# Per-token convolution taps softmaxed once in their own slots, and turned into band matrices by 32x32 transposes

## The chip, the cores and the metric

The kernel runs on one core of a Trainium2 chip. The metric is the time of one execution on the device, in microseconds (us). A core has a matrix engine (PE, with its weight loads shown apart as PEld), three engines for elementwise work (DVE, ACT, POOL) and a queue, SP, that issues the DMA transfers. Each engine works through its own list of instructions in order; semaphores make one engine wait for another.

## What is computed

Two steps over 8 sequences of 3584 tokens with 192 channels. First a dynamic convolution: each token and head has its own 7 taps, softmaxed over the 7, and mixes the token with the 6 before it in the same sequence.

```python
w = weight_gen - np.max(weight_gen, axis=-1, keepdims=True)
w = np.exp(w)
w = w / (np.sum(w, axis=-1, keepdims=True) + 1e-09)
x_unf = x_pad[:, idx, :].reshape(B, S, K, H, group)     # B 8, S 3584, K 7, H 8, group 24
out = np.einsum('bshk,bskhg->bshg', w, x_unf).reshape(B, S, D)
```

Then a soft mixture of experts over all 28672 tokens: `logits = x @ phi` (32 slots), a softmax over the tokens gives each slot's input, 8 experts (192 to 1024 to 192, ReLU) transform 4 slots each, and a softmax over the slots gives each token its mix of the outputs. All data are fp32.

## The kernel before

**Tiling.** Tokens are cut into blocks of T = 26, four blocks make a group of 104 tokens, and a sequence has 35 groups (the last one overlaps, its repeats are zeroed later), 280 in all. Two groups are a pair, two pairs a slot of the loop (`SLOTS` = 70), and eight pairs a unit (two short units of six at the end). A block with its 6 tokens of history fills 32 rows of a quarter of the partitions; the four quarters hold four heads.

**Convolution of a pair.** `conv` multiplies, for each block, a band matrix of 128 x 26 (rows: 4 heads x 32 input tokens; columns: the output tokens; each column has its 7 taps on the diagonal band) with the block's x, laid out block-diagonally by head (`big`, called `xbd`; its other quadrants are zeroed once at the start): 16 matrix products in fp32, which the trace shows as 32 matmul instructions. The x of each head carries a 25th column of ones (GX = 25), so the product's 25th column is the sum of the unnormalised taps. `conv_sum` (ACT) reads those sums, `conv_inv` (DVE) inverts them, and `conv_out` (DVE) scales the result on its way from PSUM (`cv`) to SBUF (`tm`).

**Making a band.** The taps come from DRAM twice, once by token (26 rows of 32) and once already spread along the diagonals. `tap_top` (DVE) takes each token's maximum, `tap_spread` (POOL) lays the maxima out, and `tap_rows`, a matmul with the 0/1 matrix `near` into `pmx`, carries each maximum to the rows of the band where that token's taps stand; `tap_sub` (DVE) subtracts it, `tap_exp` (ACT) exponentiates, and `band_make` (POOL) multiplies with a mask into the band. One such chain serves a load of 7 groups (1.75 slots); there are 40.

**The rest of a slot.** `xpose` (PE) transposes the convolved pair in three pieces into `pt`, `xpose_out` (ACT) copies them to `cm`; once per unit `logits` (PE into `ls`), `top`, `newmax`, `newmax_out`, `dexp`, `dturn` and `fade` (a running maximum and exponentials over tokens), `dispatch` (PE into `acb`) and `rescale` (DVE). `soft` and `turn` prepare the softmax over slots. After the loop come the experts and the outputs, which are copied out of PSUM and written by DMA.

**What sets the order.** The opening, up to pair 1, is written by hand. Everything after goes through a planner (`op` and `model`): each operation is listed with an engine, a cost and the buffers it reads and writes; PE's and SP's order is the listed one, and for DVE, ACT and POOL the planner picks by estimated due times. So a changed cost or a changed list moves instructions on those three engines.

Of the kernel before, what the change touches and what calls it, by code (L numbers as in the profile page):

```python
# [16 lines left out]
GX = GW + 1  # L17
# [3 lines left out]
SGG = 7  # L21
# [4 lines left out]
TAPS = NBC * KT  # L26
# [15 lines left out]
def conv_soft_moe(ctx, tc, xh, wh, phi, w1a, w1b, w2, out):  # L42
# [15 lines left out]
    NXH, HBC = 5, NBC // 2  # L58
    XB = 4 * HBC * GX
    big = keep.tile([128, NXH * XB], F32, name="big")  # L60
# [43 lines left out]
    NTM, NCV, NTAP, NBAND = 2, 3, 4, 3  # L104
    xbd = big.rearrange("p (i h c) -> p i h c", i=NXH, h=4)
    HB = NBC // 2


    taps = [fix.tile([128, 2, TAPS], F32, name=f"taps{i}") for i in range(NTAP)]
    bands = [fix.tile([128, T, NBC], F32, name=f"band{i}") for i in range(NBAND)]  # L110
# [5 lines left out]

    pmx = ps_l.tile([128, 512], F32, name="pmx")
    topP = pmx[:, 0:TAPS].rearrange("p (q l) -> p q l", q=KT)
# [7 lines left out]
    one = keep.tile([128, 1], F32, name="one")  # L126
# [11 lines left out]
    V.memset(one, 1.0)  # L138
    V.memset(xbd[:, 0:2, 0], 0.0)
    G.memset(xbd[:, 0:2, 1], 0.0)  # L140
    V.memset(xbd[:, 0:2, 2], 0.0)
    A.copy(xbd[:, 0:2, 3], zero.unsqueeze(1).to_broadcast([128, 2, HBC * GX]))
    ident = keep.tile([128, 128], F32, name="ident")
    make_identity(nc, ident)
    near = keep.tile([128, 128], F32, name="near")
    G.memset(near, 1.0)
    G.affine_select(out=near, in_=near, compare_op=ALU.is_ge, fill=0.0, base=0,
                    pattern=[[1, 128]], channel_multiplier=-1)
    G.affine_select(out=near, in_=near, compare_op=ALU.is_ge, fill=0.0, base=KT - 1,
                    pattern=[[-1, 128]], channel_multiplier=1)  # L150
    mask = keep.tile([128, 1, 32], F32, name="mask")
    maskT = keep.tile([128, 1, 32], F32, name="maskT")
    mask2 = keep.tile([128, 32, 1], F32, name="mask2")
    own = keep.tile([128, KT, 1], F32, name="own")

# [7 lines left out]
    eps = keep.tile([128, 1], F32, name="eps")  # L163
    V.memset(eps, EPS)
    for t in cvs:

        A.copy(t[:, 0 : 16 * GX], one.to_broadcast([128, 16 * GX]))

    def loadx(j):

        s, part = divmod(j, 2)
        z = slice(part * HBC * GX, (part + 1) * HBC * GX)
        for h in range(4):
            SY.dma_start(xbd[32 * h : 32 * h + 32, j % NXH, h], xh[s, h, :, z])  # L174

    def loadw(s):
        SY.dma_start(taps[s % NTAP], wh[s])

    tops = {}

    def tap_top(s):

        tops[s] = pa.tile([128, NBC, 1], F32, tag="top", name=f"top{s}")
        V.tensor_reduce(out=tops[s][:, :, 0], op=ALU.max, axis=AX.X,  # L184
                        in_=taps[s % NTAP][:, 0].rearrange("p (l k) -> p l k", k=KT))

    def tap_spread(s, eng=G):

        tops[s] = pa.tile([128, KT, NBC], F32, tag="spread", name=f"spread{s}"), tops[s]
        eng.tensor_tensor(out=tops[s][0], in0=own.to_broadcast([128, KT, NBC]),  # L190
                          in1=tops[s][1].rearrange("p l o -> p o l").to_broadcast([128, KT, NBC]),
                          op=ALU.mult)

    def tap_rows(s):

        P.matmul(pmx[:, 0:TAPS], near, tops[s][0].rearrange("p q l -> p (q l)"),  # L196
                 start=True, stop=True)

    def tap_sub(s):
        r = taps[s % NTAP][:, 1]  # L200
        V.tensor_tensor(out=r, in0=r, in1=pmx[:, 0:TAPS], op=ALU.subtract)  # L201

    def tap_exp(s):
        A.activation(taps[s % NTAP][:, 1], taps[s % NTAP][:, 1], AF.Exp)  # L204

    def band_make(s, lo=0, hi=HB, eng=G):

        l = slice(2 * lo, 2 * hi)
        r = taps[s % NTAP][:, 1].rearrange("p (q l) -> p q l", q=KT)[:, :, l]
        w = bands[s % NBAND]  # L210
        for j, n in ((0, 3 * KT), (3 * KT, T - 3 * KT)):
            k = min(n, KT)
            eng.tensor_tensor(out=w[:, j : j + n, l].rearrange("p (a k) l -> p a k l", k=k),  # L213
                              in0=r[:, 0:k].unsqueeze(1).to_broadcast([128, n // k, k, 2 * (hi - lo)]),
                              in1=mask2[:, j : j + n].rearrange("p (a k) o -> p a k o", k=k)
                              .to_broadcast([128, n // k, k, 2 * (hi - lo)]), op=ALU.mult)
# [11 lines left out]
    def conv(p):  # L228
        cv = cvs[p % NCV]
        for par in range(2):  # L230
            s, g = divmod(2 * p + par, SGG)
            for c in range(2):
                for blk in range(4):
                    bc = (4 * g + blk) * 2 + c
                    o = 4 * GX * (2 * par + (c ^ par))
                    j, b = divmod(s * NBC + bc, HBC)
                    P.matmul(cv[32 * blk : 32 * blk + T, o : o + 4 * GX],  # L237
                             bands[s % NBAND][:, :, bc],
                             xbd[:, j % NXH, :, b * GX : (b + 1) * GX], start=True, stop=True)

    wss = {}

    def conv_sum(p):

# [706 lines left out]
```

## Time and profile before

| | |
|---|---|
| time, median of 3 runs | 343.48 us (343.11 to 344.02) |
| the profiled execution, first to last instruction | 345.3 us |
| PE, share of the span with a matmul | 89% |
| DVE, POOL, ACT | 72%, 58%, 47% |
| conv loop (first conv to last) | about 8.6 to 258.3 us |
| experts | about 267 to 282 us |
| output writes | about 284 to 345 us |

The profile page gives only the span of the profiled execution; what may lie around it in a timed run is not on the page, and the span is 1.8 us above the median of the runs. Its rows read: line, engine, operation, output tile <- input tiles, shapes, xcount, then busy time, mean ns of one instruction, and the idle time before the instructions with what ended it. Busy time counts overlapping instructions once, so count times mean can be more than busy.

### The profile page before, as it was taken

To read this page: it belongs to the slowest core of one execution; us is meant where nothing else is said; L and a number is where in the kernel's file an instruction comes from. 1 tells how busy PE (TensorE), PEld (TensorE's weight loads), DVE (VectorE), ACT (ScalarE), POOL (GpSimd) and SP (SyncE) were. 2 spreads that over 40 slices of the span, in tenths; PEclk is the share of its full clock that TensorE was granted. 3 is DMA by queue.
4 is the path that set the end of the run, shared out by engine and by line. 5 is a ranking of instruction groups with operands and counts; after the bars stand their busy time and mean duration, and the time that the engine had idled before them with its cause. 6 is when DMAs were issued, how large, how long until landed. Compare 5 with 4: busy or idle time off the path is not lost.

```text
span 345.3 us, 16352 instructions
## 1 busy us (share of the span) xinstructions
PE 306.8 (89%) x6896; PEld 222.2 (64%) x6896; DVE 249.9 (72%) x550; ACT 161.7 (47%) x428; POOL 198.8 (58%) x261
## 2 busy tenths in 40 slices
PE   8789999899999998999999999899997988799600
PEld 6567777687778876778778777678784952124100
DVE  7766877878788886897887868777864759965400
ACT  6535454455645654456445544454632237534300
POOL 8679648679489785868778568586601720000000
PEclk9999999999999999999999999999999999975555
DMA  6787788877877777677876867966589009999995
GB/s 197 215 260 196 214 223 196 246 205 221 215 217 228 211 235 189 199 207 205 241 210 176 237 173 204 260 172 180 154 307 364 6 2 398 395 403 399 395 404 204
DMA packets 33001, 80.82 MB, mean 234 GB/s; under 512 B 7072, under 2 KB 7456, under 8 KB 32928
## 3 DMA queue, kind: packets, MB, share of 16 engines
q1 hardware_dynamic: 32928, 79.77, 74.7%
q8 instruction: 55, 0.90, 1.2%
q14 instruction: 18, 0.15, 0.2%
HBM read 57.38 MB, written 22.36 MB: 231 GB/s over the span
## 4 chain that ended last, share of the span: by engine, by line
PE 58%; DMA 19%; DVE 9%; ACT 4%; issue 3%; SPq 2%; POOL 1%; DVEq 0%; ACTq 0%; POOLq 0%
PE cv L237 25%; PE pt L272 12%; DMA taps<-wh 8%; DMA out<-big 7%; PE pmx L196 6%; PE ls L301 6%; PE acb L365 5%; DMA big<-xh 4%; DVE big L841 3%; PE hpb L765 2%; PE so L786 2%; DVE cT L455 1%; DVE top L184 1%; SPq L174 1%; DVE tm L258 1%
## 5 line engine op out<-in xcount | busy, mean ns | idle before, releaser
L213 POOL TENSOR_TENSOR band<-taps,mask 128x588 f32<-128x588 f32 (+3 forms) x158 | 121.3, 798 | 31.9 <-ACT taps L204 23.1
L237 PE MATMUL cv<-big,band 128*26 128x100 f32 x4480 | 120.4, 252 | 6.2 <-POOL band L213 1.5
L237 PEld LDWEIGHTS cv<-big,band 128*26 128x26 f32 x4480 | 101.0, 128 | 36.4 <-issue 29.0
L258 DVE TENSOR_TENSOR tm<-cv,ws 128x384 f32<-128x384 f32 x140 | 72.9, 551 | 6.7 <-DVE ws L253 1.0
L277 ACT COPY cm<-pt 128x312 f32<-128x312 f32 x140 | 51.9, 423 | 44.5 <-PE pt L272 44.0
L247 ACT ACTIVATE ws<-cv,eps 128x16 f32<-128x16 f32 x140 | 37.7, 272 | 58.0 <-PE cv L237 46.2
L272 PE MATMUL pt<-ident,tm 122*128 122x122 f32 x420 | 59.2, 277 | 0.7 <-ACT cm L277 0.7
L272 PEld LDWEIGHTS pt<-ident,tm 122*128 122x128 f32 x420 | 43.4, 141 | 16.4 <-issue 9.9
L253 DVE RECIPROCAL ws<-ws 128x32 f32<-128x32 f32 x70 | 24.3, 348 | 29.9 <-ACT ws L247 29.4
L190 POOL TENSOR_TENSOR spread<-own,top 128x392 f32<-128x392 f32 x37 | 31.2, 843 | 24.3 <-DVE top L184 13.0
L834 PE MATMUL po<-cT,so 32*128 32x468 f32 (+3 forms) x256 | 38.1, 726 | 5.2 <-DVE big L841 4.5
L841 ACT COPY big<-po 128x936 f32<-128x936 f32 (+2 forms) x25 | 22.4, 902 | 27.1 <-PE po L834 15.2
L196 PE MATMUL pmx<-spread,near 128*128 128x392 f32 x80 | 33.7, 503 | 1.6 <-POOL spread L190 0.8
L841 DVE COPY big<-po 128x884 f32<-128x884 f32 (+2 forms) x24 | 25.4, 1071 | 12.8 <-DMA out<-big 10.5
L834 PEld LDWEIGHTS po<-cT,so 32*128 32x128 f32 (+1 forms) x256 | 12.4, 188 | 29.7 <-DVE big L841 23.1
L184 DVE TENSOR_REDUCE top<-taps 128x56 f32<-128x392 f32 x40 | 22.1, 551 | 12.3 <-DMA taps<-wh 11.2
L301 PE MATMUL ls<-cm,phi_sb 128*32 128x208 f32 (+1 forms) x576 | 29.5, 334 | 0.3 <-issue 0.3
L204 ACT ACTIVATE taps<-taps 128x392 f32<-128x392 f32 x40 | 21.0, 525 | 17.5 <-DVE taps L201 14.5
L365 PE MATMUL acb<-tm,dt 128*32 128x193 f32 x536 | 26.6, 328 | 0.7 <-DVE dt L346 0.4
L301 PEld LDWEIGHTS ls<-cm,phi_sb 128*32 128x32 f32 x576 | 19.9, 109 | 4.6 <-issue 0.6
L201 DVE TENSOR_TENSOR taps<-taps,pmx 128x392 f32<-128x392 f32 x40 | 22.1, 553 | 0.4 <-PE pmx L196 0.4
L92 POOL TENSOR_TENSOR LT<-LT,sm 128x576 f32<-128x576 f32 (+1 forms) x16 | 18.1, 1132 | 5.1 <-DVE sm L90 4.9
(113 smaller groups left out, 256.0 us busy)
## 6 DMA issues: line engine op xcount, KB each, us to landing
big<-xh SPq DMA_DIRECT2D x320, 87.5 KB, 3.9
taps<-wh SPq DMA_DIRECT2D x40, 392.0 KB, 4.6
out<-big SPq DMA_DIRECT2D x23, 468.0 KB, 6.5
out<-big SPq DMA_DIRECT2D x24, 442.0 KB, 6.4
big<-w SPq DMA_DIRECT2D x8, 768.0 KB, 6.9
w1a_sb<-w1a SPq DMA_DIRECT2D x16, 256.0 KB, 3.9
w1b_sb<-w1b SPq DMA_DIRECT2D x8, 256.0 KB, 3.7
out<-big SPq DMA_DIRECT2D x2, 234.0 KB, 2.4
```

Of the source, the lines that this page charges most:

```text
L190: eng.tensor_tensor(out=tops[s][0], in0=own.to_broadcast([128, KT, NBC]), in1=tops[s][1].rearrange("p l o -> p o l").to_broadcast([128, KT ...
L196: P.matmul(pmx[:, 0:TAPS], near, tops[s][0].rearrange("p q l -> p (q l)"), start=True, stop=True)
L213: eng.tensor_tensor(out=w[:, j : j + n, l].rearrange("p (a k) l -> p a k l", k=k), in0=r[:, 0:k].unsqueeze(1).to_broadcast([128, n // k, k ...
L237: P.matmul(cv[32 * blk : 32 * blk + T, o : o + 4 * GX], bands[s % NBAND][:, :, bc], xbd[:, j % NXH, :, b * GX : (b + 1) * GX], start=True, ...
L247: A.activation(wss[p // 2][:, p % 2], cvs[p % NCV][:, 0 : 16 * GX].rearrange("p (h w) -> p h w", w=GX)[:, :, GW:], AF.Identity, bias=eps[: ...
L258: V.tensor_tensor(out=tms[u % NTM][:, pr, 1 : 2 * D + 1].rearrange("p (h w) -> p h w", w=GW), in0=cv[:, :, 0:GW], in1=wss[p // 2][:, p % 2 ...
L272: P.transpose(pt[:, i, 0:TR], tm[0:TR, pr, 1 + 128 * i : 129 + 128 * i], ident[0:TR, 0:TR])
L277: copy(cms[u][:, pr].rearrange("p i b j -> p (i b) j"), pts.pop(p).rearrange("p i (b j) -> p (i b) j", j=32)[:, :, 0:T])
L301: P.matmul(lp[32 * blk : 32 * blk + 32, 0:n, par, 0:T], phi_sb[:, 2 * par + i, :], cm[:, 0:n, 1 if i else 2 * par, blk, :], start=(i == 0) ...
L365: P.matmul(ac[32 * q : 32 * q + 32], dt[:, g, :], tm[:, g // 2, o : o + D + 1], start=(g < 4), stop=(g + 4 >= 2 * n))
L834: P.matmul(po[dst : dst + hi - lo, at, 0 : n * T], so[32 * q : 32 * q + 32, lo:hi], cT[32 * q : 32 * q + 32, g0 : g0 + n, 0:T], start=True ...
L841: (V.tensor_copy if done[1] % 2 else A.copy)(ot.rearrange("p (q c) -> p q c", c=n * T), po[:, 0 : len(qs), 0 : n * T])
```

## The change

**Taps.** They are loaded once, as [partition = head and slot of a group, 2 x 7 taps x 26 tokens]; a load ("chunk", CH = 2) serves 8 groups, two slots of the loop, and there are 35. An eighth row, set to 1e-9 once, stands in for the epsilon of the sum. Per chunk the chain is now `tap_top` (DVE), `tap_sub` (POOL), `tap_exp` (ACT), `tap_sum` (three adds on POOL, folding eight rows to one), `tap_inv` (DVE), `tap_mul` (POOL; writes the softmaxed taps into `wide` at a stride of 33 elements, so that tap k of token j stands at column k + j of row j of a 32 x 32 block), and `tap_turn` (DVE; 32x32 transposes of 128 x 1664 elements from `wide` into the band). `near`, `mask`, `own`, `tap_spread`, `tap_rows` with `pmx`, and `band_make` are gone. `wide` is one buffer; its zeros outside the bands are set once.

**Convolution.** x has no column of ones (24 columns a head, 96 instead of 100 per matmul), `conv_sum` and `conv_inv` are gone, and `conv_out` is a plain copy on ACT. There are four `cv` buffers in place of three. x is loaded by 5 groups (SGG = 5, four buffers) instead of by halves of 7 groups (five buffers): 224 transfers of 32 x 960 elements instead of 320 of 32 x 700.

**Opening.** The first chunk goes through the chain in two halves (LO, HI), partly on DVE; the zeroing of the later x buffers (`clear`) is spread over DVE, POOL and ACT between these steps. The weights of the experts' second layer (`loadw2`) go into x buffers as the last four fall free. In the planner, `dispatch` stands behind a slot's transposes, and for the unit before the first short one it comes a slot later.

```diff
+    def tap_sub(c, b=ALL, eng=G):
+        t = taps[c % NTAP][:, b, 0:KT]
+        eng.tensor_tensor(out=t, in0=t, in1=each(tops.pop((c, b.start)), b.stop - b.start),
+                          op=ALU.subtract)
+    def tap_sum(c, b=ALL, eng=None):
...
+        eng.tensor_tensor(out=s, in0=t[:, :, 0:4], in1=t[:, :, 4:8], op=ALU.add)
+        eng.tensor_tensor(out=s[:, :, 0:2], in0=s[:, :, 0:2], in1=s[:, :, 2:4], op=ALU.add)
+        eng.tensor_tensor(out=m, in0=s[:, :, 0], in1=s[:, :, 1], op=ALU.add)
+    def tap_mul(c, b=ALL, eng=G):
...
+        dst = bass.AP(w.tensor, w.offset, [w.ap[0], [T * 32, n], [1, KT], [33, T]])
+        eng.tensor_tensor(out=dst, in0=taps[c % NTAP][:, b, 0:KT],
+                          in1=each(m, n), op=ALU.mult)
+    def tap_turn(c, b=ALL):
+        V.transpose(bands[c % NBAND][:, b].rearrange("p b j l -> p (b j l)"),
+                    wide[:, b].rearrange("p b j -> p (b j)"))
...
-    def conv_sum(p):
-    def conv_inv(k):
-    def conv_out(p):
...
-        V.tensor_tensor(out=tms[u % NTM][:, pr, 1 : 2 * D + 1].rearrange("p (h w) -> p h w", w=GW),
-                        in0=cv[:, :, 0:GW], in1=wss[p // 2][:, p % 2].to_broadcast([128, 16, GW]),
-                        op=ALU.mult)
+    def conv_out(p, copy=A.copy):
+        copy(tms[u % NTM][:, pr, 1 : 2 * D + 1], cvs[p % NCV][:, 0 : 2 * D])
...
     loadw(0)
+    loadx(0)
     loadw(1)
...
+    tap_top(0, LO)
+    tap_sub(0, LO, V)
+    tap_exp(0, LO)
+    tap_top(0, HI)
+    tap_sub(0, HI)
+    clear_cv(0)
     tap_top(1)
+    tap_exp(0, HI)
+    clear_cv(1)
+    G.memset(wide[:, 0], 0.0)
+    tap_sum(0, LO)
+    tap_inv(0, LO)
+    tap_mul(0, LO, V)
+    tap_sub(1)
+    G.memset(wide[:, 1], 0.0)
+    tap_turn(0, LO)
+    tap_exp(1)
...
+    tap_sum(1, ALL, G)
+    make_identity(nc, ident)
+    clear(2, 2, G)
+    tap_inv(1)
+    tap_mul(1, LO)
+    tap_mul(1, HI)
...
+    clear(2, 3, G)
...
+    loadx(2)
+    for h in range(4):
+        clear(3, h, G)
+    loadx(3)
...
-            dispatched[k0 + 3 if n == UP else k0 + 2] = u - 1
+            dispatched[k0 + 3] = u - 1
...
+    def chain(c):
+        w = ("w", c % NTAP)
+        op(VE, 0.56, [w], [("top", c % 2)], tap_top, c)
+        op(PO, 0.85, [("top", c % 2)], [w], tap_sub, c)
+        op(AC, 0.47, [], [w], tap_exp, c)
+        op(PO, 1.05, [w], [("sum", c % 2), "fold"], tap_sum, c, ALL, G)
+        op(VE, 0.5, [], [("sum", c % 2)], tap_inv, c)
+        op(PO, 0.85, [("sum", c % 2), w], ["wide"], tap_mul, c)
+        op(VE, 1.88, ["wide"], [("band", c % NBAND)], tap_turn, c)
...
+                if t + NXS < NSG:
+                    op(SP, 2.0, [], [x_of(t)], loadx, t + NXS, late=3.0)
+                else:
+                    i = t + NXS - NSG
+                    op(SP, 1.2, [], [x_of(t)], loadw2, i * XB // WE, min((i + 1) * XB // WE, E))
...
-        steps = [(xpose, a - 2), (xpose, b - 2)] + ([(tap_rows, rowed[k])] if k in rowed else [])
...
+        for i in (a - 2, b - 2):
+            op(TE, 0.34, [tm_of(i)], [("pt", i % 2)], xpose, i)
+            op(AC, 0.4, [], [("pt", i % 2), ("cm", unit(i)[1])], xpose_out, i)
```

**Where instructions move.** On PE, slots 4 and 5 of the loop, counted from 0. `cv` is the convolution, `pt` the transposes, `pmx` the matmul of the maxima, `ls` the logits. Before:

```order
L237 MATMUL cv_96<-big,band_90 26x100 x16
L237 MATMUL cv_94<-big,band_90 26x100 x16
L272 MATMUL pt_504<-ident,tm_91 128x122 x3
L272 MATMUL pt_511<-ident,tm_91 128x122 x3
L196 MATMUL pmx<-spread_500,near 128x392
L237 MATMUL cv_95<-big,band_90 26x100 x8
L237 MATMUL cv_95<-big,band_88 26x100 x8
L237 MATMUL cv_96<-big,band_88 26x100 x16
L301 MATMUL ls<-cm_324,phi_sb 32x8x26 x16
```

and now:

```order
L231 MATMUL cv_95<-big,band_91 26x96 x16
L231 MATMUL cv_96<-big,band_91 26x96 x16
L249 MATMUL pt_472<-ident,tm_92 128x122 x3
L249 MATMUL pt_481<-ident,tm_92 128x122 x3
L231 MATMUL cv_97<-big,band_91 26x96 x16
L231 MATMUL cv_98<-big,band_91 26x96 x16
L278 MATMUL ls<-cm_305,phi_sb 32x8x26 x16
```

The `pmx` matmul is gone, a pair no longer straddles two bands, and the rest of PE's order is kept but for `dispatch`, which now follows a slot's transposes and stood ahead of them.

On DVE, the stretch around the first running maximum (`mx` and `mq` are `top`, `nm` is `newmax_out`, `dt` is `dturn`, `LT` is `save`). Before:

```order
L308 TENSOR_REDUCE mx_596<-ls 128x1
L310 TENSOR_SCALAR mq<-acb,mx_596 128x4
L258 TENSOR_TENSOR tm_92<-cv_96,ws_557 128x384
L328 TENSOR_REDUCE nm_647<-acb 128x1
L330 TENSOR_TENSOR mq<-nm_647,acb 128x1
L253 RECIPROCAL ws_644<-ws_644 128x32
L258 TENSOR_TENSOR tm_92<-cv_94,ws_644 128x384
L346 STREAM_TRANSPOSE dt_690<-dd 128x512
```

and now:

```order
L196 RECIPROCAL sum_0_523<-sum_0_523 128x52
L285 TENSOR_REDUCE mx_552<-ls 128x1
L287 TENSOR_SCALAR mq<-acb,mx_552 128x4
L209 STREAM_TRANSPOSE band_90<-wide 128x1664
L305 TENSOR_REDUCE nm_635<-acb 128x1
L307 TENSOR_TENSOR mq<-nm_635,acb 128x1
L196 RECIPROCAL sum_0_578<-sum_0_578 128x52
L323 STREAM_TRANSPOSE dt_660<-dd 128x512
```

The scalings and inversions of pairs have left; the long transposes of the band now stand between `top` and `newmax_out`, and the inversion ahead of `mx` waits for POOL's sums.

On POOL in the opening, from the sums of the second chunk to the band of the third:

```order
L192 TENSOR_TENSOR sum_0_171<-si 128x52
masks.py:197 MEMSET ident 128x128
masks.py:199 AFFINE_SELECT ident<-ident 128x128
L358 MEMSET big 128x960
L204 TENSOR_TENSOR wide<-taps_85,sum_0_171 128x7x26 x2
L358 MEMSET big 128x960 x5
L420 MEMSET selE_126 128x128
L421 MEMSET dd 128x384
...
L176 TENSOR_TENSOR taps_86<-taps_86,top_0_278 128x2x182
L176 TENSOR_TENSOR taps_87<-taps_87,top_0_301 128x2x182
L190 TENSOR_TENSOR si<-taps_86 128x208
L191 TENSOR_TENSOR si<-si 128x2x52
```

Before, the same stretch held the zeroing of x (five `MEMSET` instructions) and then at once the bands of loads 1 and 2; now six of the zeroing instructions of the third and fourth x buffer stand around the products of the second chunk and ahead of the third chunk's subtraction.

More of the change, by code (lines that the diff above doesn't have):

```diff
@@ L137, in conv_soft_moe @@
     warm(0)
[L138 to L142, printed above, removed]
-    ident = keep.tile([128, 128], F32, name="ident")
[L144 to L154, printed above, removed]
+    ident = keep.tile([128, 128], F32, name="ident")
+    eps = keep.tile([128, 1], F32, name="eps")
+    V.memset(xbd[:, 0, 0], 0.0)
+    G.memset(xbd[:, 0, 1], 0.0)
+    A.copy(xbd[:, 0, 2], zero.to_broadcast([128, NBC * GW]))
+    V.memset(xbd[:, 0, 3], 0.0)
+    for t in taps:
+        V.memset(t[:, :, KT], EPS)
+    V.memset(eps, EPS)
     sel4 = keep.tile([128, 4, NS], F32, name="sel4")
@@ L194, in tap_rows, with loadx @@
[L194 to L216, printed above, removed]
+    def loadx(t):
+        for h in range(4):
+            SY.dma_start(xbd[32 * h : 32 * h + 32, t % NXS, h], xh[t, h])
@@ L556, in conv_soft_moe @@
[L556 to L565 removed]
+            op(TE, 0.75 if p == a else 0.72, conv_reads(p), [("cv", p % NCV)], conv, p)
```

278 lines of the change are left out of this document (106 added, 172 removed).

## The prediction

> **What bounds the kernel now.** I read the summary first, then the busy times of the long middle of the program, then the chain of waits there, and last the durations by shape.
>
> ```profile
> span 345.3 us, 16352 instructions
> PE 306.8 (89%) x6896; PEld 222.2 (64%) x6896; DVE 249.9 (72%) x550; ACT 161.7 (47%) x428; POOL 198.8 (58%) x261
> ```
>
> No engine is full over the span, but the share averages an opening, a loop and an output stage that is limited by its writes. The conv loop decides. Its first regular slot (slot 4, counted from 0) starts at 24.06 us, its last convolution ends at 258.34. The row for that stretch, with busy us of PE, PEld, DVE, ACT and POOL in this order, then clock, DMA share and GB/s:
>
> ```profile
> 24.06:258.34 234.28, 228.48 (x5878) 178.89 (x5878) 185.38 (x438) 118.72 (x354) 169.80 (x209) 1.00 0.76 212
> ```
>
> PE works 228.5 of 234.3 us (97.5%), DVE 79%, POOL 72%, ACT 51%. 66 slots in 234.3 us make 3.55 us a slot. The chain of waits in the loop, in order of time (start, us, what), runs on PE from one piece to the next without a gap:
>
> ```profile
> 107.79 1.31 PE acb L365 x24
> 109.10 0.78 PE pt L272 x6
> 109.88 0.67 PE pmx L196 x2
> 110.54 1.54 PE cv L237 x64
> 112.08 0.77 PE pt L272 x6
> 112.86 1.70 PE cv L237 x64
> 114.56 1.41 PE ls L301 x32
> ```
>
> So a slot costs PE 1.54 us of convolution and 0.78 of transposes, a unit's logits (ls) 1.41 and its dispatch (acb) 1.31, and each maxima matmul (pmx) 0.67 that nothing overlaps. How many of each there are says the grouping of the same stretch by line:
>
> ```profile
> L196 PE MATMUL pmx<-spread,near 128*128 128x392 f32 x71 | 29.6, 497 | 0.8 <-POOL spread L190 0.8
> L301 PE MATMUL ls<-cm,phi_sb 128*32 128x208 f32 (+1 forms) x544 | 27.8, 336 | 0.0
> L365 PE MATMUL acb<-tm,dt 128*32 128x193 f32 x512 | 24.9, 328 | 0.7 <-DVE dt L346 0.4 <-issue 0.2
> L324 PE MATMUL acb<-mq,sel 128*32 128x5 f32 (+1 forms) x136 | 3.8, 173 | 1.0 <-DVE mq L310 1.0
> ```
>
> That is 35 pmx of two records (the 71st is cut by the window's edge), 17 logits, 16 dispatches. 66 x 2.32 + 17 x 1.41 + 16 x 1.31 + 3.8 + 35 x 0.67 = 153.1 + 24.0 + 21.0 + 3.8 + 23.5 = 225.4 us. The other 8.9 us are waits.
>
> **The change, part by part.** *PE loses the maxima matmul*: 35 x 0.67 = **23.5 us** of the loop, straight off the bound if nothing else takes its place. (By the group's busy time, which counts overlap with its neighbours, it would be 29.6; the chain's 0.67 is what the next convolution waits.)
>
> *The convolution narrows from 100 to 96 columns.* ls takes 1.41 / 32 = 44 ns an instruction for 208 columns, acb 1.31 / 32 = 41 ns for 193: both 0.212 ns a column. At that rate 100 columns would take 21 ns; the convolution takes 1.54 / 64 = 24.1. Something other than columns paces it, so I count **0**. The ends are a gain of 4% of 66 x 1.54, 4.1 us, and, since the weights are now read at a step of 32 elements instead of 56, which no row shows, a loss of as much.
> The Trainium skill (TensorE: Matmul & The Clock Gate, section "Wait — 56ns, not 53.3ns?") says that matmuls never start closer than about 25 ns, however few columns they have. By that rule the narrowing brings nothing, which goes with the 24.1; without it the sum would be 4.1 us lower.
>
> *The other engines.* Durations by shape (busy, mean ns of one):
>
> ```profile
> L258 DVE TENSOR_TENSOR tm<-cv,ws 128x384 f32<-128x384 f32 x140 | 72.9, 551 | 6.7 <-DVE ws L253 1.0
> L253 DVE RECIPROCAL ws<-ws 128x32 f32<-128x32 f32 x70 | 24.3, 348 | 29.9 <-ACT ws L247 29.4
> L90 DVE RECIPROCAL sm<-sm 128x18 f32<-128x18 f32 x8 | 2.1, 262 | 1.7 <-ACT sm L88 1.5
> L201 DVE TENSOR_TENSOR taps<-taps,pmx 128x392 f32<-128x392 f32 x40 | 22.1, 553 | 0.4 <-PE pmx L196 0.4
> L184 DVE TENSOR_REDUCE top<-taps 128x56 f32<-128x392 f32 x40 | 22.1, 551 | 12.3 <-DMA taps<-wh 11.2 <-POOL band L213 1.1
> L346 DVE STREAM_TRANSPOSE dt<-dd 128x512 f32<-128x512 f32 x16 | 11.3, 706 | 0.2
> L390 DVE STREAM_TRANSPOSE maskT<-mask 128x32 f32<-128x32 f32 x1 | 0.2, 206 | 0.0
> L308 DVE TENSOR_REDUCE mx<-ls 128x1 f32<-128x416 f32 x16 | 9.3, 581 | 1.1 <-PE ls L301 1.0
> L310 DVE TENSOR_SCALAR mq<-acb,mx 128x4 f32<-128x4 f32 x17 | 3.8, 222 | 0.6
> L277 ACT COPY cm<-pt 128x312 f32<-128x312 f32 x140 | 51.9, 423 | 44.5 <-PE pt L272 44.0
> L841 ACT COPY big<-po 128x936 f32<-128x936 f32 x12 | 11.3, 939 | 9.3 <-PE po L834 5.2 <-DMA out<-big 4.0
> L247 ACT ACTIVATE ws<-cv,eps 128x16 f32<-128x16 f32 x140 | 37.7, 272 | 58.0 <-PE cv L237 46.2 <-PE acb L324 5.3 <-DVE taps L201 3.7
> L204 ACT ACTIVATE taps<-taps 128x392 f32<-128x392 f32 x40 | 21.0, 525 | 17.5 <-DVE taps L201 14.5 <-DMA big<-xh 2.8
> L213 POOL TENSOR_TENSOR band<-taps,mask 128x588 f32<-128x588 f32 x77 | 91.0, 1182 | 31.6 <-ACT taps L204 22.8 <-issue 8.1
> L213 POOL TENSOR_TENSOR band<-taps,mask 128x140 f32<-128x140 f32 x77 | 32.6, 423 | 0.0
> L190 POOL TENSOR_TENSOR spread<-own,top 128x392 f32<-128x392 f32 x37 | 31.2, 843 | 24.3 <-DVE top L184 13.0 <-DMA big<-xh 4.2 <-PE acb L324 4.2
> ```
>
> DVE loses in the loop 132 scalings, 66 inversions, 35 subtractions and 35 maxima: 72.7 + 23.0 + 19.4 + 19.3 = 134 us. It gets, for each of 33 chunks, a maximum over 364 elements (0.55, as for 392), an inversion of 52 (6.1 ns an element between 18 and 32: 0.47) and a transpose of 1664 (1.04 ns an element between 32 and 512: 706 + 1152 x 1.04 = 1.90 us): 2.92 x 33 = 96. It ends near 147 of some 210 us, 70%. ACT loses 132 x 0.272 + 35 x 0.525 = 54 and gets 132 copies of 384 (0.827 ns an element between 312 and 936: 0.48) and 33 exponentials of 364 (0.50): 80; near 145, 69%. POOL loses 35 spreads and 35 double bands of two instructions a half (29.5 + 112.4) and gets, at 186 ns + 1.69 an element (from 140 and 588), a subtraction and a product of 364 (0.80 each) and adds of 208, 104 and 52 (0.54 + 0.36 + 0.27): 2.77 x 33 = 91; near 119, 57%. No row has a POOL write at a stride of 33. I take 0.80; the other end, twice that, puts POOL at 70%, still covered. All these lie beside PE, and cost nothing as long as PE's own queue of work hides them.
>
> A chunk's chain, 0.55 + 0.80 + 0.50 + 1.17 + 0.47 + 0.80 + 1.90 = 6.2 us, has four slots, 12.7 us, before its band is needed. DMA gets lighter: taps once instead of twice, and fewer, larger transfers of x. The last expert's weights (w2) now wait for the last x buffer, that is for the end of the convolutions at 258.3 in the old times.
>
> ```profile
> big<-w SPq DMA_DIRECT2D x8, 768.0 KB, 6.9
> 275.32 1.30 PE so L786 x32
> ```
>
> They land in 6.9 us, and the product that reads them begins 17 us after the last convolution, with the other experts first: hidden, by 10 us. `dispatch` behind the transposes instead of ahead is the same work for PE.
>
> *Waits.* Of the 8.9 us, 0.8 (pmx on spread, above) leave with the matmul. The rest I keep: 8.1.
>
> *The opening.* Rows of before in order of time (start, us):
>
> ```profile
> 0.81 0.86 SPq L177 DMA_DIRECT2D taps<-wh  x2
> 2.48 4.09 SPq L174 DMA_DIRECT2D big<-xh  x8
> 4.11 0.55 DVE L184 TENSOR_REDUCE top<-taps 128x56 f32<-128x392 f32 x1
> 7.09 1.26 POOL L396 MEMSET big<- 128x1400 f32 x1
> 8.30 1.30 POOL L398 MEMSET big<- 128x700 f32 x2
> 8.56 0.92 PE L237 MATMUL cv<-big,band 128*26 128x100 f32 x32
> 13.62 0.20 POOL L430 MEMSET selE<- 128x128 f32 x1
> 14.35 0.48 POOL L436 MEMSET qneg<- 32x1 f32 x4
> ```
>
> Taps land 3.3 us after their issue. The second chunk's are now issued behind four x transfers (0.5 each, and they wait for zeroed buffers), near 4.0, and land near 7.3; DVE has that chunk's maximum listed ahead of the first half's sums, so it stands until then. 0.55, then sum 0.36, inversion 0.31, product 0.36 and transpose 1.04 of a half bring the first convolution to about 10.0 (8.56 before); the second half follows at 12.0, the second chunk's inversion at 12.5. Behind it stand, on POOL, two products (0.5 each, 13.5), five zeroings of 960 (0.89 each by the 700 and 1400 above, 18.0), the small ones (13.62 to 14.83 above, 1.2: 19.2), two subtractions (20.8), the sums (22.0), after the inversion (0.5) the product (23.3); then DVE's transpose (25.2). Slot 4 waits for it: 25.3 against 24.06, **+1.2**. Ends: -1.5 if taps land as soon as they can and POOL takes a tenth less, +4 if a transfer of the fourth x buffer, issued at 18, is late.
>
> **Sum**: 345.3 - 23.5 - 0.8 + 1.2 = 322.2 for the profiled execution. That execution was 1.8 us above the median of the runs (343.48), so **320.5 us** for the time, 6.7% less.
>
> **Rivals.** *New waits in the loop* (330): running maxima need `top`, 0.58 + 0.22 us, within the 1.55 us that PE spends on transposes and one convolution after the logits. A 1.90 us transpose that has just begun when the logits end makes PE wait up to 1.15 us; 17 units, at most 19.6. ACT, with 69% on PE's own path (convolution, copy, transposes), can do alike. For: both instructions sit where they didn't. Against: DVE's share falls, and in the order shown the transpose follows `mq`. Half of the most, +9.8.
>
> *Less than counted* (312): the convolution gains its 4.1 and half of the waits go, since DVE and POOL have more slack.
>
> *The matmul's time isn't won* (336): PE drops its 23.5 us, but the loop is paced by what feeds it, say the chunk's chain across three engines, and keeps two thirds of it. Against: 97.5% PE.
>
> *Slower* (355): POOL's product at stride 33 is far dearer than 0.80. Two slots now take 2 x (201.9 + 8.1) / 66 = 6.4 us; POOL has besides the product 1.97 a chunk and (169.8 - 141.9) / 33 = 0.85 of other work. From 3.5 us on the product sets the pace, from 4.3 us (two slots in 7.1 us, as before) the loop is no faster than it was. At 4.6 us it takes 33 x 7.42 = 244.9 instead of 210.0: 322.2 + 34.9 - 1.8 = 355. Against: that is 12.6 ns an element, and spreads (843 ns for 392) take 2.15.
>
> **How the numbers follow.** Forecast 0.60, new waits 0.17, less than counted 0.12, not won 0.06, slower 0.05. The likeliest gives 320.5. The range, 311 to 331, takes in the third case and most of the second. 0.3% (1.0 us) is what a measurement here can tell: faster 0.94, the same 0.01, slower 0.05.
>
> **What would show it.** Right: pmx gone from PE; PE busy over 95% between slot 4 and the last convolution, 208 to 213 us apart; 64 convolution matmuls still near 1.54 us; the long transpose at 1.9 us; POOL's product near 0.8 us; the first convolution near 10 us, slot 4 near 25; after the last convolution still 87 us. Wrong: waits of PE on the logits' maximum or on ACT's copies that sum to over 10 us, or a POOL product over 3.5 us.

## The result and the profile after

The changed kernel takes 323.17 us (median of 4, 320.73 to 324.01) against 343.75 for the kernel before on the same chip (343.11 to 345.85, 4 runs): ratio 0.9375 [0.9328, 0.9422]. The forecast was 320.5, inside a range of 311 to 331. The number held; the experiments show that its reason held only in part.

The first two rows of the page of the kernel after:

```profile
span 319.0 us, 15477 instructions
PE 272.7 (85%) x6816; PEld 210.1 (66%) x6816; DVE 220.8 (69%) x366; ACT 185.5 (58%) x425; POOL 154.7 (49%) x236
```

This execution had a time of 320.73, 1.7 us above its span and the shortest of the four. By the same 1.7 the one on the page of before, with its span of 345.3, took about 347.0 (an estimate), more than any of the four above. So the spans, 26.3 us apart, and the loops overstate what the medians tell, 20.6. Now the loop, from the start of slot 4 to the end of the last convolution (busy us of PE, PEld, DVE, ACT, POOL, then clock, DMA share, GB/s), and a piece of the chain of waits in it (start, us, what):

```profile
29.60:232.70 203.10, 200.71 (x5807) 167.66 (x5808) 158.98 (x265) 140.97 (x350) 124.93 (x182) 0.99 0.69 200
```
```profile
104.52 1.32 PE cv L231 x64
105.83 0.78 PE pt L249 x6
106.61 1.48 PE cv L231 x64
108.09 1.41 PE ls L278 x32
```

The loop fell from 234.3 us to 203.1. The pmx pieces are gone, the convolution of a slot takes 1.48 instead of 1.54, transposes and logits are what they were, and PE is busy for 98.8% of the loop. What lies after the last convolution takes 86.3 us (87.0 before). The opening went the other way: slot 4 starts at 29.60 instead of 24.06.

The durations that the forecast had to guess, grouped by shape (busy, mean ns of one, idle before):

```profile
L209 DVE STREAM_TRANSPOSE band<-wide 128x1664 f32<-128x1664 f32 x33 | 62.5, 1894 | 2.6 <-POOL wide L204 2.6
L204 POOL TENSOR_TENSOR wide<-taps,sum 128x364 f32<-128x364 f32 x33 | 30.4, 920 | 18.6 <-DVE sum L196 16.4 <-DVE band L209 2.0
L176 POOL TENSOR_TENSOR taps<-taps,top 128x364 f32<-128x364 f32 x34 | 30.6, 902 | 27.2 <-DVE top L172 27.1
L172 DVE TENSOR_REDUCE top<-taps 128x52 f32<-128x364 f32 x34 | 28.7, 844 | 11.7 <-DMA taps<-wh 11.7
```

The transpose (1.90 forecast) came as worked out, as did the inversion and ACT's copy (464 and 482 ns). POOL's product at stride 33 costs 0.92, so the slower rival, which needed 4.3, is out. The maximum is the miss: 844 ns for 364 elements, where 392 took 551. DVE is 78% busy in the loop, not 70%.

### The profile page after: what moved, and what is told of

It reads as the page before. It is cut to its first block, busy times and chain, and to the rows that moved or that the text cites. A ratio compares the mean times of both kernels' runs of the same rounds, so it can differ in the third digit from the quotient of the medians.

```text
span 319.0 us, 15477 instructions
## 1 busy us (share of the span) xinstructions
PE 272.7 (85%) x6816; PEld 210.1 (66%) x6816; DVE 220.8 (69%) x366; ACT 185.5 (58%) x425; POOL 154.7 (49%) x236
## 4 chain that ended last, share of the span: by engine, by line
PE 62%; DMA 13%; DVE 10%; POOL 4%; issue 3%; ACT 2%; SPq 0%; ACTq 0%; DVEq 0%; POOLq 0%
PE cv L231 28%; PE pt L249 14%; DMA out<-big 8%; PE ls L278 7%; PE acb L342 7%; DMA taps<-wh 5%; DVE band L209 2%; DVE big L808 2%; PE hpb L732 2%; PE so L753 2%; DVE top L172 1%; POOL big L358 1%; DVE cT L445 1%; POOL wide L204 1%; ACT big L808 1%
## 5 line engine op out<-in xcount | busy, mean ns | idle before, releaser
L231 PE MATMUL cv<-big,band 128*26 128x96 f32 x4480 | 117.5, 255 | 10.8 <-POOL si L190 4.4
L237 ACT COPY tm<-cv 128x384 f32<-128x384 f32 x140 | 67.2, 482 | 43.0 <-PE cv L231 40.0
L209 DVE STREAM_TRANSPOSE band<-wide 128x1664 f32<-128x1664 f32 (+1 forms) x37 | 66.6, 1801 | 3.4 <-POOL wide L204 3.3
L176 POOL TENSOR_TENSOR taps<-taps,top 128x364 f32<-128x364 f32 (+1 forms) x35 | 31.1, 892 | 29.0 <-DVE top L172 29.0
L204 POOL TENSOR_TENSOR wide<-taps,sum 128x364 f32<-128x364 f32 (+1 forms) x35 | 31.4, 899 | 19.6 <-DVE sum L196 17.5
L172 DVE TENSOR_REDUCE top<-taps 128x52 f32<-128x364 f32 (+1 forms) x36 | 29.6, 821 | 11.7 <-DMA taps<-wh 11.7
L278 PE MATMUL ls<-cm,phi_sb 128*32 128x208 f32 (+1 forms) x576 | 29.2, 334 | 0.4 <-issue 0.4
L190 POOL TENSOR_TENSOR si<-taps 128x208 f32<-128x208 f32 x34 | 21.6, 635 | 14.1 <-ACT taps L181 13.8
L196 DVE RECIPROCAL sum<-sum 128x52 f32<-128x52 f32 (+1 forms) x36 | 16.4, 456 | 15.3 <-POOL sum L192 15.1
L181 ACT ACTIVATE taps<-taps 128x364 f32<-128x364 f32 (+1 forms) x36 | 18.3, 507 | 8.3 <-POOL taps L176 7.4
L81 POOL TENSOR_TENSOR LT<-LT,rm 128x576 f32<-128x576 f32 (+1 forms) x16 | 18.1, 1135 | 5.1 <-DVE rm L79 4.8
```

The lines of the kernel that those rows point to most:

```text
L172: V.tensor_reduce(out=m, in_=seven(taps[c % NTAP][:, b, 0:KT]), axis=AX.X, op=ALU.max)
L176: eng.tensor_tensor(out=t, in0=t, in1=each(tops.pop((c, b.start)), b.stop - b.start), op=ALU.subtract)
L204: eng.tensor_tensor(out=dst, in0=taps[c % NTAP][:, b, 0:KT], in1=each(m, n), op=ALU.mult)
L209: V.transpose(bands[c % NBAND][:, b].rearrange("p b j l -> p (b j l)"), wide[:, b].rearrange("p b j -> p (b j)"))
L231: P.matmul(cv[32 * blk : 32 * blk + T, o : o + 4 * GW], bands[g // 8 % NBAND][:, g // 4 % CH, :, i], xbd[:, t % NXS, :, b * GW : (b + 1) * ...
L237: copy(tms[u % NTM][:, pr, 1 : 2 * D + 1], cvs[p % NCV][:, 0 : 2 * D])
```

## Experiments

Loops are measured as above, from slot 4 to the last convolution. Theory A is the forecast's: PE alone sets the pace, and what PE sheds comes off the time. B says that the engines that feed PE set it. C says that several stand at the bound together. Each expectation spells out its own numbers, and some name other theories (in the opening, O is an order of queues and C the clock). Every ratio is to the kernel before as it ran in the same set (medians of 344.4 to 346.0 us), so times of different sets compare best by their ratios.

### Taking the parts out of the kernel before

**The maxima matmul alone.** In the first kernel the subtraction takes the maxima from `spread` in SBUF; in the second it goes on reading the matmul's bank, so that DVE's work is as before.

```diff
# e1_before_no_maxima_matmul
-        P.matmul(pmx[:, 0:TAPS], near, tops[s][0].rearrange("p q l -> p (q l)"), ...)
-        V.tensor_tensor(out=r, in0=r, in1=pmx[:, 0:TAPS], op=ALU.subtract)
+        V.tensor_tensor(out=r, in0=r, in1=tops[s][0].rearrange("p q l -> p (q l)"), op=ALU.subtract)
# e9_before_matmul_left_out
     def tap_rows(s):
+        if s > 1:
+            return
```

> The kernel before, without its maxima matmul: the subtraction on DVE takes the spread maxima straight from SBUF instead of from PSUM, so every other engine keeps its work (the maxima are not carried to the right rows: that part of the computation is left out). Theory A, PE's own work sets the pace of the loop: 35 x 0.67 us leave the loop, which falls from 234.3 to 210-212 us, and the time from 343.75 to 319-322 us. Theory B, the work of DVE and POOL that feeds PE sets the pace, and the change won by making that lighter: less than 8 us, a time above 335 us.

> The kernel before with the maxima matmul left out from the third group on; the subtraction on DVE still reads the matmul's bank, which keeps the second group's values, so its price stays 553 ns (the softmax is then wrong for those groups). The spread on POOL stays. Theory A (PE alone sets the pace of the loop): 38 matmuls of 0.67 us leave the 345, about 34 of them in the loop, so 320 to 323. Theory B (what feeds PE, that is DVE, POOL and ACT, sets the pace): 343 to 345. Theory C (both stand near the bound, and each gives only what the other has to spare): 335 to 342.

The first took 346.97 us, ratio 1.0032 [0.9982, 1.0082], but it is not clean: its subtraction, with both inputs in SBUF, rose to 802 ns on the mean from the 553 that it took with one input in PSUM.

```profile
L200 DVE TENSOR_TENSOR taps<-taps,spread 128x392 f32<-128x392 f32 x40 | 32.1, 802 | 0.0
```

The second is clean (the constant that it subtracts is one for all seven taps of a token, so the softmax stays as it was, other than the expectation says): 346.12 us, ratio **1.0008** [0.9976, 1.0040], where A asked for 320 to 323. Its loop (window, then the longest waits of PE and of SP's queue in it):

```profile
25.56:256.95 231.39, 212.46 (x5808) 175.39 (x5808) 184.15 (x438) 119.05 (x355) 169.13 (x208) 1.00 0.76 222
```
```profile
PE cv L239 <- issue: 9.9, 9, 2.0
PE cv L239 <- DVE tm L260: 4.5, 6, 1.7
```

The loop is 2.9 us shorter, but slot 4 starts 1.5 later and the end takes 1.0 more, so nothing is left in the time. The matmul's 29.2 us of PE's busy time are gone, and yet busy time falls only by 16.0 (228.5 to 212.5): the convolutions, the same matmuls as before, are now spread over 119.5 us instead of 112.5, so that part of the waiting counts as busy. The rest of it is mostly "issue", which names nothing that the profile shows. PE at 97.5% was no proof that its work could be taken off the time. A falls; B's 343 to 345 is nearest (the kernel before took 346.02 beside it), and C had asked for 335 to 342.

**DVE's scaling alone, and both.**

```diff
# e10_before_plain_copy; e11_before_both has the edit of e9 besides
     def conv_out(p):
...
-        V.tensor_tensor(out=tms[u % NTM][...], in0=cv[:, :, 0:GW],
-                        in1=wss[p // 2][:, p % 2].to_broadcast([128, 16, GW]), op=ALU.mult)
+        A.copy(tms[u % NTM][...], cv[:, :, 0:GW])
...
-    conv_sum(0)
-    conv_inv(0)
```

> The kernel before with its matmul, but the convolution's result is copied by ACT without the division by its sum (as in the changed kernel): DVE loses 140 products of 551 ns and 70 inversions of 348, about 101 us, ACT loses 140 sums of 272 ns and gets 140 copies of 480, about 29 us more. Nothing divides, so the tokens are not normalised. Theory A: 342 to 345, since PE has the same work. Theory B: 315 to 325. Theory C: 335 to 342.

> Both edits of the two kernels above: no maxima matmul from the third group on, and ACT's plain copy in place of sum, inversion and product. Theory A: as without the matmul, 320 to 323. Theory B: as with the plain copy, 315 to 325. Theory C: the two gains together are more than their sum, 318 to 328, where each alone gives under 10 us.

The copy alone: 342.94 us, ratio 0.9863 [0.9792, 0.9933]. Both: 338.70, ratio 0.9772 [0.9685, 0.9858]. Relief of DVE is worth 1.4%, which speaks against B (315 to 325); the time lies in A's range and just above C's. Both together are worth 2.3%, some 8 us, where each of the three theories asked for at least 18. So something stood at the bound that none of them named. The loop with both edits: its window, PE's longest waits, SP's, DVE's, and a stretch of the chain:

```profile
21.36:249.25 227.89, 207.12 (x5808) 170.98 (x5808) 102.74 (x242) 144.85 (x360) 171.14 (x210) 1.00 0.78 225
```
```profile
PE cv L239 <- DMA big<-xh: 7.9, 7, 2.6
PE cv L239 <- issue: 6.1, 8, 1.4
...
SPq L174 <- DMA taps<-wh: 15.6, 16, 2.6
...
DVE top L184 <- DMA taps<-wh: 30.7, 17, 4.5
```
```profile
124.76 0.79 PE pt L273 x6
125.55 0.09 SPq L174
...
126.62 4.21 DMA big<-xh
...
130.96 0.47 PE cv L239 x10
```

DVE is down to 45% of the loop and PE waits all the same: for x. Line 174 issues x, line 177 the taps, on one queue. There x transfers stood 15.6 us until taps had landed, and at 125.5 the chain leaves PE, goes over SP's issues and one transfer of 4.21 us, and comes back 5.4 us later. The kernel before already had the row on SP's queue; the one after has lost it, and its SP waits for PE instead, that is for buffers to be read empty:

```profile
SPq L174 <- DMA taps<-wh: 14.9, 17, 2.2
SPq L174 <- PE cv L237: 12.7, 20, 1.3
```
```profile
SPq L155 <- PE cv L231: 38.8, 28, 3.4
```

**Theory D: the transfers.** One more edit, on top of the two: the taps are loaded once, as the change does. All work of the engines stays, POOL's bands too.

```diff
# e12_before_both_taps_once
-        SY.dma_start(taps[s % NTAP], wh[s])
+        SY.dma_start(taps[s % NTAP][:, 1], wh[s][:, 1])
...
-                        in_=taps[s % NTAP][:, 0].rearrange("p (l k) -> p l k", k=KT))
+                        in_=taps[s % NTAP][:, 1].rearrange("p (l k) -> p l k", k=KT))
```

> The kernel before without the maxima matmul from the third group on and with ACT's plain copy, as in the run before this one (338.7), and besides with the taps loaded once: only the half laid out by rows, 196 KB a group instead of 392, and the maximum is taken over that half (it is then another constant, and nothing divides). All instructions of the engines stay, POOL's bands (171 us of the loop) among them; the transfers shrink by 40 x 196 KB = 7.8 of 80.8 MB. In the run before this one PE waited for x transfers and SP's queue for taps to land. Theory C (PE and the vector engines alone): no change, 336 to 341. Theory D (the transfers are the third bound): the loop falls from 228 us to 205 to 216, the time to 316 to 327. Theory E (POOL's band chain is the third bound): 335 to 341, with PE's waits then on the bands.

324.00 us (323.01 to 328.76), ratio **0.9384** [0.9296, 0.9471]; the loop is 214.7 us. D said 316 to 327 and 205 to 216.

```profile
21.07:235.75 214.68, 204.09 (x5808) 169.58 (x5808) 101.97 (x240) 144.13 (x357) 170.92 (x210) 1.00 0.69 195
```
```profile
PE cv L239 <- DMA big<-xh: 4.8, 5, 1.3
PE cv L239 <- POOL spread L190: 2.0, 1, 2.0
PE cv L239 <- issue: 1.8, 5, 0.7
...
SPq L174 <- DMA taps<-wh: 2.3, 6, 0.5
```

Halving the taps' bytes brings 13.2 us of loop, with POOL at the same 171 us (so E, POOL's bands, isn't the third bound). The wait of SP's queue on the taps falls from 15.6 to 2.3 us. Whether it is the bytes or the time that x stands behind the taps on the queue is left open: the DMA engines were not full in any of these loops (0.78 at most), and both shrank together. The loop's ledger, from before to after, each loop from one execution: without the matmul 2.9 us; without DVE's scaling as well, 3.5 more; with the taps loaded once as well, 13.2 more; and 11.6 between that kernel and the one after. Of the last, about 4 are the convolution's (66 slots at 1.48 instead of 1.54); the rest, new bands and fewer, larger x transfers among them, wasn't taken apart. Whether loading the taps once helps alone, with matmul and scaling in place, wasn't run either: this ledger holds for this order of the steps.

### Loading the kernel after

**A matmul put back, and PE's work cut.** The first adds to every second slot a matmul of 128x384 into a bank that the next convolution overwrites; the second multiplies half of the columns.

```diff
# e4_after_plus_matmul
+        P.matmul(cvs[p % NCV][:, 0 : 2 * D].rearrange("p (a b) -> p a b", b=128), ident,
+                 ident.unsqueeze(1).to_broadcast([128, 3, 128]), start=True, stop=True)
...
+        if k % 2 == 0 and k + 1 < SLOTS - 2:
+            op(TE, 0.67, [], [("cv", (b + 1) % NCV)], again, b + 1)
# e3_after_48_columns
-                             xbd[:, t % NXS, :, b * GW : (b + 1) * GW], start=True, stop=True)
+                             xbd[:, t % NXS, :, b * GW : b * GW + GW // 2], start=True, stop=True)
```

> The kernel after, with one matmul more in every second slot, 33 of 128 x 384, at the place where the maxima matmul stood (its result is overwritten by the next convolution). Nothing but PE gets work. Theory A: 33 x 0.66 = 21.7 us more, a time of 343-346 us. Theory B: the matmul fits in PE's waits, less than 5 us more.

> The kernel after, its convolution matmuls over 12 of the 24 columns of a head, 48 instead of 96 (half of the convolution is left out). Columns set the price all the way down: 64 instructions take 0.74 us where 96 columns took 1.48. A floor just under 24 ns an instruction: they stay above 1.4 us. In between, the floor lies where the row stops falling. If they fall far, PE is no longer the bound and ACT's copies should appear among PE's waits.

The matmul put back: 341.81 us, ratio 0.9926 [0.9886, 0.9967], which is 18.6 us more than the kernel after, where A's sum was 21.7 and its range, 343 to 346, is just missed; the loop goes from 203.1 to 225.1. Half the columns: 322.5 in its one run, loop 204.4, although PE's busy time there fell from 200.7 to 179.7. The granted clock was 0.96 in that loop, against 0.99, and took back a part: the transposes, unchanged, were busy for 57.2 us instead of 55.0.

```profile
28.94:233.30 204.36, 179.69 (x5807) 147.39 (x5808) 158.75 (x265) 137.83 (x350) 124.48 (x182) 0.96 0.71 205
```
```profile
PE cv L231 <- issue: 10.6, 14, 1.5
PE acb L302 <- DVE mq L288: 6.6, 5, 2.8
PE acb L343 <- issue: 3.4, 2, 2.8
```

So PE's work costs most of its price when it is added and brings nothing when it leaves: it is at the bound, and others stand right behind it. The chain of the kernel after agrees. It lies on PE for 86% of the loop, but from 122.7 to 147.9 us it runs over ACT, POOL, DVE and two landings of taps (4.50 and 4.09 us), while PE waits for only 0.2 us in that stretch.

**The feed made heavier**: POOL's product runs twice and half of DVE's transpose is repeated, 0.92 + 1.03 us a chunk.

```diff
# e8_after_feed_heavier
+        op(PO, 0.85, [("sum", c % 2), w], ["wide"], tap_mul, c)
...
+        op(VE, 1.0, ["wide"], [("band", c % NBAND)], tap_turn, c, LO)
```

> The kernel after, where each chunk's product is done twice on POOL and half of its transposes twice on DVE: 0.92 and 1.04 us more for every two slots, 30 and 34 us in all, and the chunk's chain gets 2 us longer. Theory A, PE alone sets the pace: POOL rises to about 75% and DVE to about 90% of the loop, the time stays within 3 us. Theory B, the chain of the taps sets the pace: 20 us or more longer.

334.27 us, ratio 0.9728 [0.9677, 0.9779]: 11 us more, though PE's work is the same, and between the 3 that A allowed and the 20 that B asked for.

```profile
PE acb L342 <- DVE dt L323: 9.1, 9, 2.5
PE cv L231 <- DVE band L209: 8.3, 7, 5.0
```

DVE (89% busy in that loop) now holds up PE twice over, with bands and with `dt`, which stands in line behind the longer transposes. This is the mechanism of the rival "new waits in the loop"; the kernel after has 2.9 us on the band and none of note on `dt`.

**The columns.**

```diff
# e2_before_96_columns: the kernel before, without the column of ones
-                             xbd[:, j % NXH, :, b * GX : (b + 1) * GX], start=True, stop=True)
+                             xbd[:, j % NXH, :, b * GX : b * GX + GW], start=True, stop=True)
```

> The kernel before, its convolution matmuls over 96 of their 100 columns (the column of ones is not multiplied, so the taps' sums are left out and the scalings work on constants). Step by the columns: 64 convolution instructions fall from 1.54 to 1.48 us as in the kernel after, the loop by 66 x 0.06 = 4 us. A floor of 24 ns an instruction: they stay at 1.54 us, and then the kernel after has its 1.48 from the weights' closer step of 32 elements.

346.23 us in its one run, beside 345.05 for the kernel before: nothing to be seen in the time. What 64 convolution matmuls take says PE's own list (start, us from the first start to the last end), here of before (100 columns), of this kernel, of the kernel after (96) and of the one with 48:

```profile
124.16 1.60 PE L237 MATMUL cv<-big,band 128*26 128x100 f32 x64
```
```profile
124.50 1.58 PE L237 MATMUL cv<-big,band 128*26 128x96 f32 x64
```
```profile
125.23 1.55 PE L231 MATMUL cv<-big,band 128*26 128x96 f32 x64
```
```profile
108.96 1.09 PE L231 MATMUL cv<-big,band 128*26 128x48 f32 x64
```

With the last matmul's own 0.25 us (0.22 at 48 columns) taken off (the trace models these ends) and the rest shared by 63, the starts lie 21.4, 21.1, 20.6 and 13.8 ns apart on the mean; single ones come in small groups, mostly under 15 ns apart within a group. The columns do pace the convolution, but not alone: half of them leave two thirds of the distance, between the two ends that the expectation named. And of the 0.05 us between before and after, the columns alone (the second row) give 0.02 in these bursts; the other 0.03 came with what else the kernel after changes, the closer step of the weights among it, and was not taken apart.

### The opening

Three edits of the kernel after: the taps of chunk 3 are issued ahead of x's third and fourth buffers; PE is kept busy with 18 more idle matmuls before the first convolution; and both, with the fourth x buffer zeroed earlier, in gaps of DVE and POOL, and ACT's clearings ahead of its first copy.

```diff
# e5_after_taps_first
+    loadw(3)
     loadx(2)
...
     loadx(3)
-    loadw(3)
# e6_after_kept_warm
-WARM = 9, 5
+WARM = 9, 23
# e7_after_opening_reordered: both of the above, and
+    clear(3, 2, G)
...
+    clear(3, 0, V)
+    clear(3, 1, V)
...
+    clear(3, 3, G)
...
+    clear_cv(3)
+    clear(2, 1, A)
     conv_out(0)
-    clear_cv(3)
-    clear(2, 1, A)
...
-    for h in range(4):
-        clear(3, h, G)
```

> The kernel after, with the load of the fourth chunk's taps issued ahead of the third and fourth x buffer instead of behind them. Slot 4 began at 29.6 us, 4.3 later than forecast. Theory O, an order of queues: DVE stood 6.0 us for these taps (the maximum of chunk 3), POOL behind it, and chunk 2's sums behind POOL's subtraction of chunk 3. Then slot 4 begins about 2.9 us earlier, near 26.7, and the time falls by about 3 us. Theory C, the clock: PE idles 4.4 us ahead of the first convolution, its granted clock falls to 0.5 and the late start is that. Then slot 4 stays within 0.5 us of 29.6.

> The kernel after, with 18 more idle matmuls behind the 14 at the start, so that PE has no gap ahead of the first convolution. Theory C: the clock stays at 1.0, the first four pairs take 3.1 instead of 5.0 us, and slot 4 begins 2 us earlier or more. Theory O: the pairs get faster, slot 4 still begins near 29.6 since its band is as late, and the time falls by at most the 1.2 us that slot 4 itself lost at half clock.

> The kernel after with both of these, and the zeroing of the fourth x buffer moved to gaps of DVE and POOL while they wait for taps, ACT's last two clearings moved ahead of its first copy. POOL then has 3.6 us less to do between the products of chunk 1 and the sums of chunk 2. Theory O: slot 4 begins near 23.5, 6 us earlier, the time is 316-318 us. Theory C alone: 321-322 us.

| kernel | time, us | ratio to before | slot 4 starts | loop |
|---|---|---|---|---|
| after | 323.17 | 0.9375 [0.9328, 0.9422] | 29.60 | 203.1 |
| taps first | 318.79 | 0.9237 [0.9188, 0.9286] | 26.80 | 201.6 |
| kept warm | 322.51 | 0.9343 [0.9289, 0.9397] | 29.43 | 206.7 |
| reordered | **315.58** (6 runs, 314.86 to 318.27) | 0.9189 [0.9146, 0.9231] | 24.11 | 206.2 |

What holds slot 4 in the kernel after, in order of time (start, us, engine, in brackets the wait before it):

```profile
10.82 8.26 SPq L155 DMA_DIRECT2D big<-xh  x8
19.13 0.55 SPq L158 DMA_DIRECT2D taps<-wh  x1
22.86 0.84 DVE L172 TENSOR_REDUCE top<-taps 128x52 f32<-128x364 f32 x1 [5.96 <-DMA taps<-wh]
23.78 0.89 POOL L176 TENSOR_TENSOR taps<-taps,top 128x364 f32<-128x364 f32 x1 [2.92 <-DVE top L172]
24.64 0.63 POOL L190 TENSOR_TENSOR si<-taps 128x208 f32<-128x208 f32 x1
26.71 0.89 POOL L204 TENSOR_TENSOR wide<-taps,sum 128x364 f32<-128x364 f32 x1 [0.59 <-DVE sum L196]
27.63 1.91 DVE L209 STREAM_TRANSPOSE band<-wide 128x1664 f32<-128x1664 f32 x1 [1.00 <-POOL wide L204]
29.60 2.79 PE L231 MATMUL cv<-big,band 128*26 128x96 f32 x64 [2.87 <-DVE band L209]
```

The x transfers on SP's queue wait for zeroings until 19.08 (the profile puts 6.6 us of it to ACT's and 1.6 to POOL's), and the taps of chunk 3 stand behind them. DVE's maximum of that chunk comes at 22.86; POOL, in order, has its subtraction listed ahead of the sums of chunk 2, so that chunk 2, which slot 4 needs and whose taps had long been there, waits for chunk 3's. With the taps first, slot 4 starts 2.8 us sooner, where 2.9 was expected, which confirms it; the time falls by 4.4, where about 3 was expected. Keeping PE warm changes the first convolutions (64 in 1.55 us, where 128 took 5.00) and not the start of slot 4, nor the time beyond what the intervals leave open. The loops in the table are of one execution each, the longest of its kernel in the last two rows and the shortest in the first two, so their differences are not read. The reordered kernel is the fastest of all (slot 4 near 23.5 and 316 to 318 us were expected): it beats the kernel before by 8.1%, and its interval lies clear of that of the kernel after.

## Why the prediction was right, point by point

- **What bounds the kernel.** "No engine is full" and "the conv loop decides" held, and so did the count of PE's work: the loop after is nearly PE's list once more, 98.8% busy. But the step "straight off the bound if nothing else takes its place" was taken without a price for the "if". Something does take its place: the matmul out by itself gives 1.0008. That the time came out as forecast is luck in this respect: the change also lifts what would have held the loop.
- **"DMA gets lighter"** stood in the forecast as a remark, worth nothing. In the order in which the parts were taken out it is the dearest of them, 13.2 us of loop. The row of the loop before had a DMA share of 0.76, and SP's queue waited 14.9 us for taps to land. The chain said it too: the forecast showed a stretch of it that runs on PE without a gap, but over the whole loop taps landing hold 9.4% of the chain and x landing 5.9%, against 8.3% for the pmx matmuls. The pages have it by share of the span, before and after:

```profile
PE cv L237 25%; PE pt L272 12%; DMA taps<-wh 8%; DMA out<-big 7%; PE pmx L196 6%; PE ls L301 6%; PE acb L365 5%; DMA big<-xh 4%; DVE big L841 3%; PE hpb L765 2%; PE so L786 2%; DVE cT L455 1%; DVE top L184 1%; SPq L174 1%; DVE tm L258 1%
```
```profile
PE cv L231 28%; PE pt L249 14%; DMA out<-big 8%; PE ls L278 7%; PE acb L342 7%; DMA taps<-wh 5%; DVE band L209 2%; DVE big L808 2%; PE hpb L732 2%; PE so L753 2%; DVE top L172 1%; POOL big L358 1%; DVE cT L445 1%; POOL wide L204 1%; ACT big L808 1%
```

The runs show that matmul and scaling without the transfers bring 2.3%, and all three 6.2%. The 23.5 us could be had because the change lifts transfers (49.6 to 40.6 MB in the loop), DVE and PE together.
- **The convolution at 0.** Wrong by the end that the forecast had as its bound: 66 x 0.06 = 4.0 us. The failed step divided 1.54 us by 64 and took 24.1 ns for a pace. The starts lie 21.4 ns apart on the mean, which is about what 100 columns ask at 0.212 ns each; the rest of the 1.54 is one fixed part a burst, 1.54 - 63 x 0.0214 = 0.19 us. How much of the 4.0 is the columns' and how much came with the rest of the change stays open (above). The Trainium skill (TensorE: Matmul & The Clock Gate, "Wait — 56ns, not 53.3ns?") has matmuls never start closer than about 25 ns; the starts here, 20.6 ns apart on the mean at 96 columns and 13.8 at 48, do not agree with it.
- **Waits kept at 8.1.** The forecast's own sum of pieces, with what they take now, gives 66 x 2.26 + 17 x 1.41 + 16 x 1.29 + 4.0 = 197.8 us (a slot with a dispatch takes 1.45 + 1.32 where the others take 1.48), so 5.3 of the 203.1 are waits. That, and the convolution's 4.0, put the loop 6.9 us under the 210.0.
- **The opening at +1.2.** It was +5.5. The forecast followed POOL's list, but put chunk 3's subtraction there without asking when its taps arrive, behind two x buffers on SP's queue. It had the place and named a late x transfer as its +4 end; the late one was a taps transfer. Two pieces of the first half on DVE, its sum and its product, took 0.56 and 0.48 us where 0.36 each was put.
- **Costs on the other engines.** In the loop right within 0.12 us except the maximum, 0.84 for 0.55: priced by its element count, while it now reads seven taps 26 elements apart. No wait of PE in the loop was seen to hang on it; in the opening its 0.3 us lie on the way to slot 4.
- **The sum.** The span was put at 322.2 and was 319.0: loop -6.9, opening +4.3, the end -0.7. The median then lies 4.2 us above this span, where the forecast took 1.8 off, setting the span of one execution beside the times of others. So errors of 3.2 and 6.0 us in opposite directions cancel to 2.7 us of 320.5: the closeness is luck too.
- **The rivals.** "The matmul's time isn't won" had the right idea, a loop paced by what feeds it, but looked for it in the chunk's chain across engines, not in the transfers, and gave it 0.06. "Less than counted" had two of its parts come true, the convolution and the waits, and the opening took them back.

## What to carry to other kernels

A row with PE at 97% says that PE is late last, not what follows when it is relieved: before its time is taken off, read the DMA share and the waits of the queue that issues the loads, and ask how far the loop could shrink at the transfer rate that it already has. When several resources stand close together, an edit pays only with its companions (here 0%, 1.4%, 2.3%, then 6.2% with the third), and putting one of them back took 18.6 of the 20.6 us. In an opening, follow every buffer back to the issue of its transfer and to what stands ahead of it on the queue.

## What the runs showed of the hardware

- The same subtraction on DVE took 553 ns with one input in PSUM and 802 with both in SBUF, while POOL was busy with its own SBUF products. With PSUM the 40 of them lay between 544 and 565 ns, without it between 523 and 1537, so the dearer ones are not dear by themselves. The Trainium skill (SBUF — State Buffer, "Who interferes with whom") says that such an instruction contends with POOL's reads; the row agrees, though no run here took POOL away.
- A maximum over seven elements, 364 in all, took 844 ns when they lay 26 elements apart, and 551 ns for 392 when they lay side by side.
- The granted clock fell to half for part of the opening after PE had been idle for 4.4 us, and not in the reordered kernel, where PE had been kept busy (slices of the span in tenths, first of the kernel after, then of the reordered one), and the first convolutions of 64 took about 2.5 us instead of 1.56.

```profile
PEclk9587999999999999999999999999999999985555
```
```profile
PEclk9999999999899999999999999999999999985555
```
